# An MLP pair behind top-k attention on one core: second-GEMM products issued by PSUM bank

## The chip, the cores and the metric

The kernel runs on one core of one Trainium2 chip. The metric is the device time of one execution in microseconds. Three runs of the kernel before took 1196.57, 1201.1 and 1203.75 us; the median is 1201.1 us.

## The reference

Attention with a top-32 mask runs over 4 batches, 8 heads, 576 positions and a head size of 64. Its output, 2304 tokens of 512 columns, goes through two MLPs one after the other, each 512 to 2048 to 512: the first with softplus, the second with `h - tanh(h)`.

```python
scores = (q @ k.T) / sqrt(64)
kth = the 32nd largest score of each row
attn = softmax(where(scores >= kth, scores, -1e9)) @ v
x = attn as (2304, 512)
h = x @ moe_w_in;   y = softplus(h) @ moe_w_out
h = y @ moe2_w_in;  out = (h - tanh(h)) @ moe2_w_out
```

All inputs and the output are float32.

## The kernel before

Float32 operands are split into a high and a low float16 part, and each product of the two MLPs becomes three matmuls: high by high, high by low, low by high.

Tokens come in ten chunks: eight of 256 tokens (two per batch, from the plan at line 30) and two of 128, which hold the 64 positions of each batch that are left over. Attention is worked tile by tile, 128 rows of one head at a time: `front` (L1082) makes scores on TensorE and copies them to SBUF on ScalarE, `chain` (L1100) finds the 32 largest on VectorE, `exps`, `mask` and `turn` (L1114 to L1144) make the weights and transpose them by DMA into `pT`, and `back` (L1146) multiplies with the values into the PSUM tile `px`.

Each chunk then has sixteen MLP steps: `m` is 0 or 1 for the first or second MLP, and `g` runs over eight groups of 256 of the 2048 inner columns. `mlp_step` (L1341) calls `gemm1` (L1215, into the PSUM tile `h`), then `act1` (L1232: ScalarE, VectorE for the second MLP, and GpSimd make the two halves of `g`), and puts the step on the list `pend`. `run_gemm2` (L1322) takes it from there three or four steps later and calls `gemm2` (L1254). Gemm2 adds into the accumulators `acc`, PSUM tiles named `y`: two banks for a chunk of 256 tokens, one for 128. In the first MLP a bank holds two blocks of 128 output columns, by 256 tokens; in the second it holds 128 tokens, by all 512 output columns. After `g = 7` the first MLP calls `y_finish` (L1282): ScalarE squares each bank in turn with a running sum, a small matmul adds the sums over partitions, VectorE makes a scale from it, and ScalarE and VectorE write the high and low parts of the next input, bank by bank. The second MLP calls `out_finish` (L1306): a scaled copy of each bank and its DMA out.

The order on each engine is not the order of these calls. A `Recorder` (L149) notes every operation with its cost, its inputs and its outputs, and `order` (L432) lays them out with a model of five engines, in five turns from which the shortest plan is kept; each turn ranks the operations by how late they may start. Everything recorded inside `nc.burst()` (L169) on TensorE is one operation to the planner: it is placed as a whole, starts when all of its inputs are there, and its results count as ready when it ends. TensorE operations that have been ready for 500 ns (`MARG`, L97) come first. On the chip each instruction waits by itself for what it reads. `idle` (L455) adds filler matmuls (L525) in gaps that the plan shows, after 200 us, to hold the clock up. Before about 240 us the kernel also converts the weights, which arrive as float64 words; no gemm2 runs until then.

In gemm2 a burst is one half `fb` (128 inner columns) of a step, over all banks:

```python
for fb in range(2):
    with nc.burst():
        ...
            for d in range(ND):          # m == 0: 4 blocks x 3 matmuls of 256
        ...
            for tt in range(T // P):     # m == 1: 2 banks x 3 matmuls of 512
```

Of the kernel before, what the change touches and what calls it, by code (L numbers as in the profile page):

```python
# [9 lines left out]
F32 = mybir.dt.float32  # L10
F32R = mybir.dt.float32r
BF16 = mybir.dt.bfloat16
F16 = mybir.dt.float16
I32 = mybir.dt.int32
AF = mybir.ActivationFunctionType
ALU = mybir.AluOpType
AX = mybir.AxisListType
# [7 lines left out]
STEP = float(2.0**90)  # L25
# [16 lines left out]
KE = 'P'  # L42
NQH = 1
OWN = 3
MINC = 1
HPW = 100
HPW2 = 0
# [484 lines left out]
def topk_attention_two_mlps(  # L532
# [37 lines left out]
    def al(tag, bufs, shape, dtype, pool=sb, cap=None):  # L570
        s = slots.setdefault(tag, [0, []])
        w = mybir.dt.size(dtype)
        n = math.prod(shape[1:]) * w // 4
        i = s[0] % bufs
        s[0] += 1
        if len(s[1]) <= i:
            s[1].append([pool.tile([P, cap or n], F32, tag=f"{tag}_{i}", name=f"{tag}_{i}"), None])
        s[1][i][1] = Gen(s[1][i][1], s[1][i][0] if pool is pb else None)
        t = View(s[1][i][0][:, 0:n], s[1][i][1])
        t = t if dtype == F32 else t.bitcast(dtype)  # L580
        if len(shape) > 2:
            names = "abcde"[: len(shape) - 1]
            t = t.rearrange(f"p ({' '.join(names)}) -> p {' '.join(names)}", **dict(zip(names, shape[1:])))
        return t
# [21 lines left out]
    def tiny(n=1):  # L606
        o = used_[0]
        used_[0] += n
        return tiles_[:, o : o + n]
# [42 lines left out]
    def xy_take(shape, dtype, name, i=None):  # L652
        if i is None:
            i = xy_free.pop(0)
        return i, al(f"xy{i}", 1, shape, dtype, cap=512)
# [200 lines left out]
    def norm(x, b, s, inv):  # L856
        xf = x[b].rearrange("h s d -> (h s d)").rearrange("(p n) -> p n", p=P)
        n = H * S * D // P
        np_ = -(-n // 512)
        w = n // np_ // 2 * 2  # L860
        ss = al("vss", 2, [P, np_], F32)
        for i in range(np_):
            o, e = i * w, (i + 1) * w if i < np_ - 1 else n
            j, st = xy_take([P, 512], F32, "vst")
            st = st[:, : e - o]
            nc.sync.dma_start(st, xf[:, o:e])
            xy_free.append(j)
            nc.scalar.activation(st, st, AF.Square, accum_out=ss[:, i : i + 1])

        def finish():  # L870
            tot = tiny()
            nc.vector.tensor_reduce(tot, ss, axis=AX.X, op=ALU.add)
            pow2_scale(col_norm(tot, 1), s, inv)
        return finish

    def v_norm(b):

        return norm(v, b, sx[b], ix[b])

    def exp_scale(iq, ik, es, nes, nst):  # L880
        nc.vector.scalar_tensor_tensor(es, iq, QK, ik, op0=ALU.mult, op1=ALU.mult)
        nc.vector.tensor_scalar(nes, es, -1.0, None, op0=ALU.mult)
        nc.vector.tensor_scalar(nst, es, -STEP, None, op0=ALU.mult)
# [10 lines left out]
    def visit_norm(vi):  # L894

        vi.sq, vi.iq, vi.sk, vi.ik, vi.es, vi.nes, vi.nst = (tiny() for _ in range(7))
        ss = al("qss", 1, [P, 2], F32)
        for u, (t, s, inv) in enumerate(((vi.q, vi.sq, vi.iq), (vi.k, vi.sk, vi.ik))):
            j, st = xy_take([P, 2 * D * t.shape[2]], F16, "nst")
            xy_free.append(j)  # L900
            nc.scalar.activation(st, t.rearrange("p j t d -> p (j t d)"), AF.Square, accum_out=ss[:, u : u + 1])
            pow2_scale(col_norm(ss[:, u : u + 1], 1), s, inv)
        exp_scale(vi.iq, vi.ik, vi.es, vi.nes, vi.nst)

    def visit_scales(vi):
# [62 lines left out]
        pass  # L968

    seen = {}  # L970

    def visit_load(b, p, ts, left, twice):
        vi = Visit()
        vi.b, vi.p, vi.ts, vi.left, vi.twice = b, p, ts, left, twice
        nt = len(ts)
        h0 = 2 * p
        vi.kT = []
        vi.again = seen.get((b, p))
        if vi.again is None:
            vi.k = al("kraw", NKR, [P, 2, NB + 1, D], F32)  # L980
            nc.gpsimd.memset(vi.k[SL:P, :, NB, :], 0.0)
            vi.v = al("v", NVR, [P, 2, NB + 1, D], F32)
            for src, dst in ((k, vi.k), (v, vi.v)):
                nc.sync.dma_start(
                    dst[:, :, 0:NB, :],
                    src[b, h0 : h0 + 2, 0 : NB * P, :].rearrange("h (p t) d -> p h t d", t=NB),
                )
                nc.sync.dma_start(dst[0:SL, :, NB, :], src[b, h0 : h0 + 2, NB * P : S, :].rearrange("h s d -> s h d"))

            nc.sync.dma_start(vi.v[SL:P, :, NB, :], v[b, h0 : h0 + 2, NB * P : S, :].rearrange("h s d -> s h d"))  # L990
        if nt:
            vi.q = al("qraw", NQR, [P, 2, nt, D], F32, cap=256)
            for j in range(2):
                nc.sync.dma_start(
                    vi.q[:, j],
                    q[b, h0 + j, 0 : NB * P, :].rearrange("(p t) d -> p t d", t=NB)[:, ts[0] : ts[0] + nt, :],
                )
        if left is not None:
            vi.ql = al("ql", 1, [P, D], F32)
            for j in range(2):  # L1000
                nc.sync.dma_start(vi.ql[j * SL : (j + 1) * SL, :], q[b, h0 + j, NB * P : S, :])
        return vi
# [212 lines left out]
    def gemm1(stp):  # L1215
        m, T, g = stp.m, stp.T, stp.g
        hi, lo = whi[2 * m], wlo[2 * m]
        ps = al("h", NH, [P, 512], F32, pb)
        for fb in range(2):
            with nc.burst():  # L1220
                o = ps[:, fb * T : (fb + 1) * T]
                for d in range(ND):
                    xhi, xlo = stp.x.block(d)[:, 0, :], stp.x.block(d)[:, 1, :]
                    f0 = g * GW + d * 256 + fb * P
                    f = slice(f0, f0 + P)
                    nc.tensor.matmul(o, hi[:, f], xhi, start=(d == 0), stop=False)
                    nc.tensor.matmul(o, hi[:, f], xlo, start=False, stop=False)
                    nc.tensor.matmul(o, lo[:, f], xhi, start=False, stop=(d == ND - 1))
        stp.h = ps[:, 0 : 2 * T]


# [22 lines left out]
    def gemm2(stp):  # L1254
        m, T, g = stp.m, stp.T, stp.g
        hi, lo = whi[2 * m + 1], wlo[2 * m + 1]
        acc = stp.acc
        last = g == NG - 1
        for fb in range(2):
            with nc.burst():  # L1260
                gh, gl = (t[:, fb * T : (fb + 1) * T] for t in (stp.ghi, stp.glo))
                f0 = g * GW + fb * DM
                if m == 0:
                    per = 512 // T
                    for d in range(ND):
                        dd = slice(f0 + d * P, f0 + (d + 1) * P)
                        o = acc[d // per][:, d % per * T : (d % per + 1) * T]
                        first = g == 0 and fb == 0 and d % per == 0
                        fin = last and fb == 1 and d % per == per - 1
                        nc.tensor.matmul(o, hi[:, dd], gh, start=first, stop=False)  # L1270
                        nc.tensor.matmul(o, hi[:, dd], gl, start=False, stop=False)
                        nc.tensor.matmul(o, lo[:, dd], gh, start=False, stop=fin)
                else:
                    f = slice(f0, f0 + DM)
                    for tt in range(T // P):
                        t = slice(tt * P, (tt + 1) * P)
                        first = g == 0 and fb == 0
                        nc.tensor.matmul(acc[tt], gh[:, t], hi[:, f], start=first, stop=False)
                        nc.tensor.matmul(acc[tt], gh[:, t], lo[:, f], start=False, stop=False)
                        nc.tensor.matmul(acc[tt], gl[:, t], hi[:, f], start=False, stop=(last and fb == 1))  # L1280

    def y_finish(ch):  # L1282
        acc = ch.acc1
# [157 lines left out]
    def prep_for(st):  # L1441
        i = st.spec["i"]
        ensure_load(i + 1)
        vi = st.spec["vi"]
        if not vi.kT:
            if i < OWN:
                visit_norm(vi)
            else:
                visit_scales(vi)
            visit_prep_k(vi)  # L1450
            visit_prep_q(vi)
        if st.kind == "l":
            visit_prep_left(vi)
# [66 lines left out]
    NT = len(tiles)  # L1520
    credit = 0.0
    v_norm_at = {12: 1, 40: 2, 56: 3}
    qk_norm_at = {4: 0, 16: 1, 44: 2, 60: 3}

    def emit_steps(n, budget):
        nonlocal_credit[0] += budget
# [39 lines left out]
    for n in range(-1, NT + 2 + BL):  # L1566
# [28 lines left out]
        if 0 <= n + 8 < NT:  # L1595
            ensure_load(tiles[n + 8].spec["i"] + 1)
        if n == VN:
            v_norm(0)()
        if cur is not None and n >= VN and not hasattr(cur.vi, "vdone"):
            with nc.ahead(HP):  # L1600
                visit_prep_v(cur.vi)
# [61 lines left out]
```

## Time and profile before

| what | value |
|---|---|
| median of three runs | 1201.1 us |
| lowest and highest run | 1196.57 and 1203.75 us |
| profiled execution, its own time | 1193.43 us |
| its span | 1191.7 us |
| mean granted clock of TensorE | 0.949 |
| instructions in the profile | 28235 |

The span runs from the first to the last recorded instruction; the time of the same execution has 1.7 us around it. All times in the rows below are microseconds from the start of the span, and a duration is that of one instruction unless a count stands behind it. PE is TensorE's matmuls, PEld its weight loads, DVE is VectorE, ACT is ScalarE, POOL is GpSimd and SP issues DMAs. Neighbouring matmuls overlap in the profile: each row's duration includes the way through the array, so the pace is read from start to start or from the chain. Nearly all instructions carry line 528, the one place from which the recorder emits them, so they are told apart by their tiles.

### The profile page before, as it was taken

To read this page: it belongs to the slowest core of one execution; us is meant where nothing else is said; L and a number is where in the kernel's file an instruction comes from. 1 tells how busy PE (TensorE), PEld (TensorE's weight loads), DVE (VectorE), ACT (ScalarE), POOL (GpSimd) and SP (SyncE) were. 2 spreads that over 40 slices of the span, in tenths; PEclk is the share of its full clock that TensorE was granted. 3 is DMA by queue.
4 is the path that set the end of the run, shared out by engine and by line. 5 is a ranking of instruction groups with operands and counts; after the bars stand their busy time and mean duration, and the time that the engine had idled before them with its cause. 6 is when DMAs were issued, how large, how long until landed. Compare 5 with 4: busy or idle time off the path is not lost.

```text
span 1191.7 us, 28235 instructions
## 1 busy us (share of the span) xinstructions
PE 1050.5 (88%) x10167; PEld 819.7 (69%) x10167; DVE 965.7 (81%) x2116; ACT 912.7 (77%) x1884; POOL 887.2 (74%) x1259
## 2 busy tenths in 40 slices
PE   3477634898998999999999999999998999999998
PEld 2234333787757776787689867986687779977965
DVE  3998999899998999979999989899799898610021
ACT  7999999968998898778887977798568676733332
POOL 3476899899998877857899779787895689643333
PEclk9778865999999999999999999999999999999999
DMA  8977987745589985635775644458555444200000
GB/s 271 283 221 212 263 241 216 176 98 104 110 165 209 186 170 120 138 69 115 145 152 107 139 90 97 88 112 149 107 111 116 78 92 83 52 7 19 1 10 18
DMA packets 322828, 153.18 MB, mean 129 GB/s; under 512 B 270208, under 2 KB 302464, under 8 KB 322688
## 3 DMA queue, kind: packets, MB, share of 16 engines
q1 hardware_dynamic: 322688, 151.39, 55.9%
q8 instruction: 79, 1.29, 0.5%
q14 instruction: 61, 0.50, 0.1%
HBM read 73.04 MB, written 15.37 MB: 74 GB/s over the span
## 4 chain that ended last, share of the span: by engine, by line
PE 37%; DVE 19%; ACT 18%; POOL 9%; DMA 9%; issue 6%; SPq 1%; ACTq 0%; POOLq 0%; DVEq 0%
PE y L528 16%; PE h L528 16%; DVE m L528 8%; DVE x L528 7%; ACT whi L528 3%; DMA pT<-hl 3%; POOL hl L528 3%; ACT ssb L528 2%; ACT x L528 2%; PE px L528 2%; ACT xy L528 2%; ACT wlo L528 2%; PE s L528 2%; ACT hl L528 1%; DMA whi<-in_moe_w_in_dram 1%
## 5 line engine op out<-in xcount | busy, mean ns | idle before, releaser
L528 PEld LDWEIGHTS <-whi 128*128 128x128 f16 x3872 | 360.5, 98 | 69.3 <-issue 13.6
L528 PE MATMUL h<-xy,whi 128*128 128x256 f16 (+1 forms) x2560 | 396.1, 263 | 3.7 <-DMA xy<-xs 2.4
L528 PE MATMUL h<-xy,wlo 128*128 128x256 f16 (+1 forms) x1280 | 325.1, 263 | 0.0
L528 DVE MAX8 m<-x 128x8 f32<-128x576 f32 x432 | 314.6, 745 | 1.6
L528 POOL TENSOR_TENSOR hl<-x,hl 128x512 f16<-128x512 f32 (+1 forms) x288 | 216.1, 769 | 40.1 <-ACT hl L528 26.8
L528 DVE MATCH_REPLACE8 x<-m,x 128x576 f32<-128x576 f32 x288 | 212.6, 739 | 0.0
L528 PEld LDWEIGHTS <-wlo 128*128 128x128 f16 x1920 | 188.2, 98 | 19.8 <-issue 1.9
L528 PE MATMUL y<-g,whi 128*128 128x256 f16 (+1 forms) x1280 | 199.5, 263 | 2.2 <-POOL g L528 1.5
L528 PE MATMUL y<-whi,g 128*128 128x512 f16 x576 | 192.2, 379 | 0.2 <-ACT r L528 0.2
L528 POOL TENSOR_TENSOR g<-r,g 128x512 f16<-128x512 f32 (+1 forms) x160 | 170.5, 1067 | 13.8 <-PE y L528 8.7
L528 PE MATMUL y<-g,wlo 128*128 128x256 f16 (+1 forms) x640 | 162.9, 263 | 0.0
L528 DVE SCALAR_TENSOR_TENSOR r<-h,hinb,r 128x512 f32<-128x512 f32 (+1 forms) x80 | 54.8, 686 | 124.1 <-ACT r L528 124.1
L528 PEld LDWEIGHTS <-g 128*128 128x128 f16 x864 | 83.2, 98 | 75.6 <-issue 0.5
L528 ACT ACTIVATE x<-ssb,nb,tiny 128x576 f32<-128x576 f32 x144 | 124.3, 867 | 14.1 <-DVE m L528 10.9
L528 DVE MAX8 m<-ssb 128x8 f32<-128x576 f32 x144 | 107.5, 747 | 16.6 <-ACT ssb L528 16.3
L528 PEld LDWEIGHTS <-pT 128*128 128x128 f16 (+1 forms) x2240 | 89.0, 102 | 46.2 <-DMA pT<-hl 20.4
L528 PE MATMUL px<-vhl,pT 128*128 128x65 f16 (+1 forms) x2240 | 96.4, 197 | 25.8 <-ACT x L528 12.7
L528 ACT CAST hl<-x 128x576 f16<-128x576 f32 x144 | 96.5, 670 | 22.4 <-POOL x L528 18.6
L528 PE MATMUL s<-kT,qT 128*128 128x288 f16 x512 | 89.3, 300 | 26.0 <-ACT ssb L528 19.5
L528 PE MATMUL y<-wlo,g 128*128 128x512 f16 x288 | 109.2, 379 | 0.0
L528 DVE MATCH_REPLACE8 x<-m,ssb 128x576 f32<-128x576 f32 x144 | 106.4, 739 | 0.0
L528 POOL TENSOR_SCALAR r<-r,gsb 128x512 f32<-128x512 f32 (+1 forms) x80 | 52.4, 655 | 66.5 <-ACT g L528 59.9
(137 smaller groups left out, 1886.8 us busy)
## 6 DMA issues: line engine op xcount, KB each, us to landing
whi<-in_moe_w_in_dram SPq DMA_DIRECT2D x8, 1024.0 KB, 6.5
wlo<-in_moe_w_in_dram SPq DMA_DIRECT2D x6, 1024.0 KB, 6.9
vd<-vhl SPq DMA_DIRECT2D x16, 330.0 KB, 3.7
vhl<-vd SPq DMA_DIRECT2D x16, 330.0 KB, 3.2
kd<-kT SPq DMA_DIRECT2D x32, 160.0 KB, 2.4
whi<-in_moe_w_out_dram SPq DMA_DIRECT2D x5, 1024.0 KB, 5.7
wlo<-in_moe_w_out_dram SPq DMA_DIRECT2D x5, 1024.0 KB, 5.2
kT<-kd SPq DMA_DIRECT2D x32, 160.0 KB, 3.0
```

The source lines that it names most:

```text
L528: fn(*a, **k)
```

## The change

In gemm2 the products are first listed as parts, each with a half `fb`, a bank `i` and the blocks in it. For 256 tokens there are four parts of 6 matmuls (first MLP) or 3 (second); for 128 tokens two of 12 or 3. In the last step of a chunk (`g = 7`) the list is sorted by bank. With `SPB = 2` each part is a burst of its own. The start flag of a bank is still set on its first product and the stop flag on its last.

Other edits of the diff are governed by constants. `OWN0`, `V0`, `EXQ` and `NSL` are 0, which leaves the former path; `G1B = 4` with `ND = 4` leaves gemm1's bursts at four blocks. In `visit_norm` the sum for k goes to column 2 of a buffer of three rather than column 1 of two; the branch for leftover rows is for visits with leftovers, which the first three visits, the only ones that come here, don't have.

```diff
+G1B = 4
+SPB = 2
...
 def gemm1(stp):
...
         for fb in range(2):
-            with nc.burst():
-                o = ps[:, fb * T : (fb + 1) * T]
-                for d in range(ND):
+            o = ps[:, fb * T : (fb + 1) * T]
+            for d0 in range(0, ND, G1B):
+                with nc.burst():
+                    for d in range(d0, min(ND, d0 + G1B)):
...
 def gemm2(stp):
...
-        for fb in range(2):
+        if m == 0:
+            per = 512 // T
+            parts = [(fb, i, range(i * per, (i + 1) * per)) for fb in range(2) for i in range(len(acc))]
+        else:
+            parts = [(fb, i, (i,)) for fb in range(2) for i in range(len(acc))]
+        if SPB and last:
+            parts.sort(key=lambda x: x[1])
+        runs = [[x] for x in parts] if SPB == 1 and (last or g == 0) or SPB == 2 else \
+            [[x for x in parts if x[0] == fb] for fb in range(2)] if not (SPB and last) else [[x for x in parts if x[1] == i] for i in range(len(acc))]
+        for run in runs:
             with nc.burst():
...
+                for fb, i, ds in run:
+                    gh, gl = (t[:, fb * T : (fb + 1) * T] for t in (stp.ghi, stp.glo))
+                    f0 = g * GW + fb * DM
+                    for d in ds:
+                        start, stop = g == 0 and fb == 0 and d == ds[0], last and fb == 1 and d == ds[-1]
+                        if m == 0:
+                            dd = slice(f0 + d * P, f0 + (d + 1) * P)
+                            o = acc[i][:, d % per * T : (d % per + 1) * T]
+                            nc.tensor.matmul(o, hi[:, dd], gh, start=start, stop=False)
+                            nc.tensor.matmul(o, hi[:, dd], gl, start=False, stop=False)
+                            nc.tensor.matmul(o, lo[:, dd], gh, start=False, stop=stop)
+                        else:
+                            f = slice(f0, f0 + DM)
+                            t = slice(i * P, (i + 1) * P)
+                            nc.tensor.matmul(acc[i], gh[:, t], hi[:, f], start=start, stop=False)
+                            nc.tensor.matmul(acc[i], gh[:, t], lo[:, f], start=False, stop=False)
+                            nc.tensor.matmul(acc[i], gl[:, t], hi[:, f], start=False, stop=stop)
```

## Rows read from the trace of the kernel before

**Rows 1.** The page: busy time by engine, and the granted clock in 40 slices.

```profile
...
PE 1050.5 (88%) x10167; PEld 819.7 (69%) x10167; DVE 965.7 (81%) x2116; ACT 912.7 (77%) x1884; POOL 887.2 (74%) x1259
...
PEclk9778865999999999999999999999999999999999
...
```

**Rows 2.** Busy time in stretches: length, PE, PEld, DVE, ACT, POOL, clock, DMA, GB/s.

```profile
...
290.20:300.90 10.70, 9.34 (x95) 7.17 (x93) 10.68 (x27) 10.15 (x25) 10.25 (x17) 0.84 0.79 158
300.90:417.70 116.80, 106.75 (x1039) 83.39 (x1036) 110.85 (x250) 104.76 (x232) 102.86 (x159) 0.99 0.79 168
417.70:426.70 9.00, 7.18 (x79) 5.73 (x77) 8.54 (x25) 9.00 (x21) 6.76 (x18) 0.81 0.85 143
426.70:530.20 103.50, 101.25 (x978) 80.40 (x976) 95.45 (x222) 82.25 (x179) 79.33 (x111) 1.00 0.58 124
530.20:538.10 7.90, 5.79 (x58) 4.43 (x57) 7.56 (x21) 7.17 (x16) 4.30 (x9) 0.78 0.33 70
538.10:909.60 371.50, 362.00 (x3861) 291.20 (x3860) 348.66 (x741) 293.48 (x596) 309.85 (x463) 1.00 0.59 117
909.60:917.90 8.30, 6.56 (x86) 5.38 (x84) 8.30 (x23) 6.82 (x16) 2.90 (x7) 1.00 0.69 121
917.90:1030.00 112.10, 112.10 (x1207) 92.47 (x1205) 97.95 (x205) 77.74 (x155) 86.68 (x118) 1.00 0.40 81
1030.00:1187.60 157.60, 157.13 (x1415) 119.52 (x1412) 23.47 (x47) 58.79 (x101) 63.25 (x85) 1.00 0.06 14
sum 947.60, PE 913.57 PEld 729.37 DVE 759.26 ACT 684.96 POOL 713.71; mean PE 91.36 PEld 72.94 DVE 75.93 ACT 68.50 POOL 71.37
...
```

**Rows 3.** Groups of instructions by form, TensorE, 240 to 1192 us: the fillers.

```profile
...
L525 PE MATMUL h<-tiny 128*128 128x256 bf16 x103 | 15.8, 305 | 0.0
...
L525 PE MATMUL px<-tiny 128*128 128x256 bf16 x39 | 5.5, 274 | 0.0
...
```

**Rows 4.** The chain of work that ended last, 1050 to 1192 us: start, length, what.

```profile
...
1127.90 1.31 PE y L528 x12
...
1177.23 9.73 PE y L528 x45
...
```

**Rows 5.** Timeline, 417.5 to 426.9 us: start, duration, engine, instruction.

```profile
...
417.56 0.27 PE L528 MATMUL y<-g,wlo 128*128 128x256 f16 x1
...
418.31 0.78 ACT L528 ACTIVATE ssb<-ssb,m 128x576 f32<-128x576 f32 x1
...
418.99 0.67 ACT L528 ACTIVATE xy<-y,icab 128x512 f16<-128x512 f32 x1
...
419.65 0.68 ACT L528 ACTIVATE xy<-y,icab 128x512 f16<-128x512 f32 x1
...
420.47 0.38 PE L528 MATMUL px<-yss,tiny 128*128 128x1 f32 x2 [0.29 <-ACT xy L528]
...
423.37 1.27 ACT L528 ACTIVATE xy<-y,sc 128x512 f16<-128x512 f32 x2
...
425.18 1.40 DVE L528 SCALAR_TENSOR_TENSOR xy<-y,sc,xy 128x512 f16<-128x512 f32 x2
...
426.71 0.38 PE L528 MATMUL h<-xy,whi 128*128 128x256 f16 x2
...
```

**Rows 6.** Timeline, 909 to 911 us: another end of a first MLP.

```profile
...
909.48 0.27 PE L528 MATMUL y<-g,wlo 128*128 128x256 f16 x1
909.48 0.67 ACT L528 ACTIVATE xy<-y,icab 128x512 f16<-128x512 f32 x1
...
910.14 0.68 ACT L528 ACTIVATE xy<-y,icab 128x512 f16<-128x512 f32 x1
...
```

**Rows 7.** TensorE's waits, 240 to 1192 us: total, times, longest.

```profile
...
PE px L528 <- DMA pT<-hl: 10.3, 13, 2.6
PE s L528 <- ACT ssb L528: 8.4, 10, 2.2
...
```

**Rows 8.** Timeline, 1186.5 to 1192 us: the output copies.

```profile
...
1187.04 1.33 ACT L528 ACTIVATE r<-y,icb 128x512 f32<-128x512 f32 x2 [6.68 <-PE y L528]
...
```

More of the change, by code (lines that the diff above doesn't have):

```diff
@@ L44 @@
 OWN = 3
+OWN0 = 0
+V0 = 0
+EXQ = 0
+G1B = 4
+NSL = 0
+NSB = 1
+SPB = 2
 MINC = 1
@@ L866, in norm @@
             nc.sync.dma_start(st, xf[:, o:e])
-            xy_free.append(j)
+            xy_free.insert(NSL - 1 if NSL and b >= NSB else len(xy_free), j)
             nc.scalar.activation(st, st, AF.Square, accum_out=ss[:, i : i + 1])
@@ L880, in exp_scale @@
     def exp_scale(iq, ik, es, nes, nst):
+        if EXQ:
+            nc.gpsimd.tensor_scalar(es, iq, ik, QK, op0=ALU.mult, op1=ALU.mult)
+            nc.gpsimd.tensor_scalar(nst, es, -STEP, 1.0, op0=ALU.mult, op1=ALU.mult)
+            nc.gpsimd.tensor_scalar(nes, es, -1.0, 1.0, op0=ALU.mult, op1=ALU.mult)
+            return
         nc.vector.scalar_tensor_tensor(es, iq, QK, ik, op0=ALU.mult, op1=ALU.mult)
@@ L896, in visit_norm @@
         vi.sq, vi.iq, vi.sk, vi.ik, vi.es, vi.nes, vi.nst = (tiny() for _ in range(7))
-        ss = al("qss", 1, [P, 2], F32)
+        ss = al("qss", 1, [P, 3], F32)
+        left = vi.left is not None
+        if vi.again is not None:
+            vi.sk, vi.ik = None, vi.again[2]
+        if left:
+            j, st = xy_take([P, D], F16, "nst")
+            xy_free.append(j)
+            nc.scalar.activation(st, vi.ql, AF.Square, accum_out=ss[:, 1:2])
         for u, (t, s, inv) in enumerate(((vi.q, vi.sq, vi.iq), (vi.k, vi.sk, vi.ik))):
+            if t is None:
+                continue
             j, st = xy_take([P, 2 * D * t.shape[2]], F16, "nst")
             xy_free.append(j)
-            nc.scalar.activation(st, t.rearrange("p j t d -> p (j t d)"), AF.Square, accum_out=ss[:, u : u + 1])
-            pow2_scale(col_norm(ss[:, u : u + 1], 1), s, inv)
+            nc.scalar.activation(st, t.rearrange("p j t d -> p (j t d)"), AF.Square, accum_out=ss[:, 2 * u : 2 * u + 1])
+            n = 2 if u == 0 and left else 1
+            pow2_scale(col_norm(ss[:, 2 * u : 2 * u + n], n), s, inv)
         exp_scale(vi.iq, vi.ik, vi.es, vi.nes, vi.nst)
@@ L970, in topk_attention_two_mlps, with first_v_load @@
     seen = {}
+    first_v = []
+    if V0:
+        for p in range(NP):
+            if p == 0:
+                x = al("v", NVR, [P, 2, NB + 1, D], F32)
+            else:
+                c = NG * GW - 2 * 2 * (NB + 1) * D * p
+                x = wlo[2][:, c : c + 2 * 2 * (NB + 1) * D].bitcast(F32).rearrange("p (h t d) -> p h t d", h=2, t=NB + 1)
+            first_v.append(x)
+    def first_v_load():
+        ss = al("vss", 2, [P, NP], F32, cap=5)
+        for p in range(NP):
+            dst = first_v[p]
+            nc.sync.dma_start(dst[:, :, 0:NB, :],
+                              v[0, 2 * p : 2 * p + 2, 0 : NB * P, :].rearrange("h (p t) d -> p h t d", t=NB))
+            for r in (slice(0, SL), slice(SL, P)):
+                nc.sync.dma_start(dst[r, :, NB, :], v[0, 2 * p : 2 * p + 2, NB * P : S, :].rearrange("h s d -> s h d"))
+            j, st = xy_take([P, 2 * (NB + 1) * D], F16, "vst")
+            xy_free.append(j)
+            nc.scalar.activation(st, dst.rearrange("p h t d -> p (h t d)"), AF.Square, accum_out=ss[:, p : p + 1])
+        tot = tiny()
+        nc.vector.tensor_reduce(tot, ss, axis=AX.X, op=ALU.add)
+        pow2_scale(col_norm(tot, 1), sx[0], ix[0])
     def visit_load(b, p, ts, left, twice):
@@ L978, in visit_load @@
         vi.again = seen.get((b, p))
+        vi.k = None
         if vi.again is None:
@@ L981, in visit_load @@
             nc.gpsimd.memset(vi.k[SL:P, :, NB, :], 0.0)
-            vi.v = al("v", NVR, [P, 2, NB + 1, D], F32)
-            for src, dst in ((k, vi.k), (v, vi.v)):
+            vi.v = first_v[p] if b == 0 and V0 else al("v", NVR, [P, 2, NB + 1, D], F32)
+            for src, dst in ((k, vi.k),) if b == 0 and V0 else ((k, vi.k), (v, vi.v)):
                 nc.sync.dma_start(
@@ L988, in visit_load @@
                 nc.sync.dma_start(dst[0:SL, :, NB, :], src[b, h0 : h0 + 2, NB * P : S, :].rearrange("h s d -> s h d"))
-            nc.sync.dma_start(vi.v[SL:P, :, NB, :], v[b, h0 : h0 + 2, NB * P : S, :].rearrange("h s d -> s h d"))
+            if b or not V0:
+                nc.sync.dma_start(vi.v[SL:P, :, NB, :], v[b, h0 : h0 + 2, NB * P : S, :].rearrange("h s d -> s h d"))
         if nt:
@@ L1219, in gemm1 @@
         for fb in range(2):
-            with nc.burst():
-                o = ps[:, fb * T : (fb + 1) * T]
-                for d in range(ND):
[L1223 to L1228, printed above, removed]
+            o = ps[:, fb * T : (fb + 1) * T]
+            for d0 in range(0, ND, G1B):
+                with nc.burst():
+                    for d in range(d0, min(ND, d0 + G1B)):
+                        xhi, xlo = stp.x.block(d)[:, 0, :], stp.x.block(d)[:, 1, :]
+                        f0 = g * GW + d * 256 + fb * P
+                        f = slice(f0, f0 + P)
+                        nc.tensor.matmul(o, hi[:, f], xhi, start=(d == 0), stop=False)
+                        nc.tensor.matmul(o, hi[:, f], xlo, start=False, stop=False)
+                        nc.tensor.matmul(o, lo[:, f], xhi, start=False, stop=(d == ND - 1))
         stp.h = ps[:, 0 : 2 * T]
@@ L1258, in gemm2 @@
         last = g == NG - 1
-        for fb in range(2):
-            with nc.burst():
[L1261 to L1280, printed above, removed]
@@ new lines, in gemm2 @@
+        for run in runs:
+            with nc.burst():
+                for fb, i, ds in run:
[9 more added lines that the diff above has]
+                            nc.tensor.matmul(o, lo[:, dd], gh, start=False, stop=stop)
+                        else:
+                            f = slice(f0, f0 + DM)
[3 more added lines that the diff above has]
+                            nc.tensor.matmul(acc[i], gl[:, t], hi[:, f], start=False, stop=stop)
@@ L1445, in prep_for @@
         if not vi.kT:
-            if i < OWN:
+            if i < OWN or OWN0 and vi.b == 0:
                 visit_norm(vi)
@@ L1522, in topk_attention_two_mlps @@
     v_norm_at = {12: 1, 40: 2, 56: 3}
-    qk_norm_at = {4: 0, 16: 1, 44: 2, 60: 3}
+    qk_norm_at = {16: 1, 44: 2, 60: 3} if OWN0 else {4: 0, 16: 1, 44: 2, 60: 3}
     def emit_steps(n, budget):
@@ L1597, in topk_attention_two_mlps @@
         if n == VN:
-            v_norm(0)()
+            if V0:
+                first_v_load()
+            else:
+                v_norm(0)()
         if cur is not None and n >= VN and not hasattr(cur.vi, "vdone"):
```

## Prediction

> **What bounds the kernel now.** I read the page first [rows 1]: TensorE is busy 88% of the span and its clock is granted in full nearly everywhere after the first fifth. Then I cut the time after 240 us into stretches [rows 2]. The products that the change touches all run in that time. From 917.9 us on TensorE is busy 112.1 of 112.1 us and 157.13 of 157.6 us, and from 538.1 to 909.6 us it is 362.0 of 371.5 us. VectorE, which finds the top-32 values, is nearly as full up to about 1030 us and then falls to 23.47 of 157.6 us. So the second half is a queue of TensorE work that never empties, and the end moves by what TensorE loses before it. Over 240 to 1187.6 us it idles 947.6 - 913.57 = 34.0 us, and issues 103 + 39 filler matmuls beside it [rows 3].
>
> Is a busy TensorE really full? In the chain of work that ended last, 45 products of 512 columns take 9.73 us (216 ns each) and 12 of 256 columns take 1.31 us (109 ns each) [rows 4]. At 2.4 GHz 512 columns are 213 ns and 256 are 107 ns, so there is no room between them. The work itself does not shrink with the change: as many matmuls and weight loads as before. Only idle time, fillers and clock can be gained.
>
> Where does it go idle? Four stretches in [rows 2] stand out: 290.2 to 300.9, 417.7 to 426.7, 530.2 to 538.1 and 909.6 to 917.9 us, 35.9 us together with 28.87 us of busy time, much of it fillers. Each lies between the last y product of a chunk's first MLP step and the first h product of its second step, when no other chunk has work ready. One of them in detail [rows 5]: the last y product starts at 417.56 us and ends 0.27 us later, at 417.83. ScalarE squares bank 0 at 418.99 and bank 1 at 419.65, the column sum follows at 420.47, the scaled copies at 423.37, VectorE's residues at 425.18, and the first h product at 426.71: 8.9 us after the last y product ended.
>
> **The change, part by part.** It does one thing that acts: the planner's atomic runs of gemm2 for 256-token chunks become half as long, 6 products of 256 columns (0.65 us instead of 1.31) in the first MLP and 3 of 512 columns (0.65 instead of 1.30) in the second [rows 4]. In the last step of a chunk all products of bank 0 come before those of bank 1. The two 128-token chunks have one bank, so their runs stay as they are. Bursts of gemm1 hold four blocks before and after, the new constants at 0 leave their branches unused, the free list is appended to as before, and one column of a small statistics buffer changes its place: nothing for any of these. No DMA is added or moved past another on SP's queue, no wait is added, and POOL's work is the same; POOL's two operations per step still come before the run.
>
> (a) Bank 0 earlier at a chunk's end. Before, bank 0 gets its last product 6 products (0.65 us) ahead of the end; after, 12 products (1.31 us). That the chip lets the square of bank 0 start by itself shows at 909.48 us, where it starts while the last y product is still starting [rows 6]. At 417.7 us it did not: an attention operation that started at 418.31 stood ahead in ScalarE's queue [rows 5]. The planner counts a burst as done when its last product is, so to it bank 0 was ready only with bank 1. With runs by bank it knows better. The least gain is that the first square and its sum (418.99 to 419.65, 0.66 us) leave the chain, if ScalarE finds the place; the most is that plus the wait from 417.83 to 418.99, 1.82 us; below nothing if the square pushes the attention's copy in front. I take 0.9 us, nearer to the 0.66 since that needs no reordering, at three of the four ends; at the fourth the square is early already, and the second can start when that product ends, 909.48 + 0.27 = 909.75, instead of 910.14: 0.4 us. Together 3 x 0.9 + 0.4 = **3.1 us** (0 to 5.9). At the other ends of 256-token chunks h products of another chunk cover it: nothing there, or the same 0.9 if that cover is gone.
>
> (b) The clock. In the first three stretches the granted share is 0.84, 0.81 and 0.78 [rows 2]. With two levels, 1.2 and 2.4 GHz, that is 0.16 x 2 x 10.7 = 3.4 us at the lower one, and as much in the others. Half of each, 1.7 us, is lost where real work runs in it. Before each drop TensorE had too little ready but fillers. A shorter stretch can save one: **1.7 us** (0 to 5.1), an estimate of one in three.
>
> (c) Attention matmuls behind gemm2. A score or output product that becomes ready waits for the run in front, now 0.65 us at most. VectorE gets its scores that much earlier, and the plan has twice the places to put them. The waits of TensorE that this could ease are those for pT and for the score copy, 10.3 + 8.4 = 18.7 us [rows 7]. Most of them are the order's guess being off and stay. I take a tenth, **1.9 us**, between 0 and half (9.4), and as far on the loss side for the reason given under the rivals.
>
> (d) The next chunk's first products can enter bank 0 while bank 1 is still read. While one chunk's bank is evacuated h runs and attention cover it; nothing, or one evacuation (0.67 us) if they are gone. (e) The end: the two output copies take 1.33 us from 1187.04 [rows 8]. Bank 0's copy moves forward, but bank 1's waits for the last product as now: 0.1 us, nothing.
>
> Sum: 3.1 + 1.7 + 1.9 = 6.7 us. The profiled execution took 1193.4 us, 7.7 below the median of the three runs, 1201.1, and below the lowest of them. I apply the sum to the median: 1201.1 - 6.7 = **1194.4 us**; against the profile's own time it would be 1186.7.
>
> **The rivals.** First, the forecast itself, faster by over 0.5%: the chunk ends shorten, and the idle time of 34.0 us falls to under 29. Its own range is 1186 to 1195.
>
> Second, no change that counts. ScalarE is full in the dry stretches: 10.15 of 10.7, 9.0 of 9.0, 7.17 of 7.9 us [rows 2]. A square that moves forward then pushes an attention copy back, and the products that wait for that copy fill the same stretch anyway. Only the fourth end's 0.4 and part of (c) remain, about 2 us: 1199. Against it: the attention operations moved back are not on the way to the first h product. That the change has no effect at all, because the planner puts the halves back to back again, belongs here: 1201.
>
> The Trainium skill (Perfetto Trace Analysis, section Identifying the Most-Contended Engine) holds matmul busy time to be a poor measure of how full TensorE is, and would have headroom judged by weight-load busy time. By that, 119.52 of 157.6 us after 1030 us would leave a quarter free, TensorE would catch up whatever it lost, and the sum would be zero: 1201. The row of 45 products without a gap [rows 4] speaks against it, so it gets 0.03 inside this case.
>
> Third, slower. TensorE takes its instructions in order. Each boundary between runs is a place where the planner may put a score or output product as soon as its model calls the inputs ready (it keeps a margin of 500 ns, the constant MARG). Where the real pT transfer comes later than that, TensorE stands while ready y and h products queue behind it, and ScalarE and VectorE wait for them in turn. The 18.7 us of [rows 7] are such waits. Gemm2 has twice the boundaries now. If the idle time grows by a third, it costs 34.0 / 3 = 11.3 us: 1212. The 13 + 10 waits of those rows are 0.81 us each in the mean, so it takes 14 more of them. Eight chunks of 16 steps get two new boundaries a step, 256 in all: the case decides once one in eighteen of them stalls, that is where pT or the score copy comes later than planned by more than the margin. For it: these waits are already the largest that TensorE has after 240 us. Against it: earlier scores also make VectorE, and so pT, earlier.
>
> **How the numbers follow.** A measurement of this kernel can tell about 0.5%, 6 us, from no change: faster is under 1195.1, slower over 1207.1. The forecast case has 0.45; no change 0.36, of it 0.04 for no effect at all and 0.03 for the busy measure; slower 0.19. The forecast lies close to the bound, so the two first cases are near each other. The range takes the forecast's lower bounds, with all three terms near their better ends (3.1 + 5.1 + 9.4 = 17.6 would be 1183.5), down to 1185, and reaches over no change into a mild loss, 1208. Most of the slower case, and a little below, is left out. Cases of both signs hold 0.64, so the likeliest one's own range stands with it above.
>
> **What would show it.** In the profile after: the square of bank 0 starts before the last y product of the chunk ends, at all four ends; the way from that product to the first h product falls from about 9 to 8 us; fillers under 142; fewer stretches at the lower clock; TensorE idle under 29 us over the same time. In runs of y products 6 or 3 at a time between attention products one sees the halves used. Wrong: TensorE's idle time unchanged with the squares early (the second case), or its waits for pT and score copies above 18.7 us (the third). A change before 240 us, where no product of gemm2 runs, would be the planner's reordering alone and none of these terms.

## The result and the profile after

The changed kernel takes 1189.53 us in the median of twelve runs (1184.65 to 1192.89), the kernel before 1200.18 us in twelve runs (1193.01 to 1203.75). The ratio is 0.9913, with a 95% interval from 0.9891 to 0.9935: 10.7 us, or 0.9%, faster. The forecast was 1194.4 us in a range of 1185 to 1208.

The profiled executions are only 4.4 us apart, 1189.07 against 1193.43 us, since the execution profiled before is nearly the fastest of its kernel. What follows from one pair of traces must be read with that in mind.

The page of the changed kernel: the span, the busy time by engine and the granted clock in 40 slices, as in [rows 1].

```profile
span 1187.0 us, 28134 instructions
...
PE 1044.8 (88%) x10121; PEld 814.4 (69%) x10121; DVE 957.4 (81%) x2116; ACT 911.4 (77%) x1884; POOL 892.7 (75%) x1259
...
PEclk9779855899999999999999999999999999999999
...
```

46 matmuls fewer have been issued, all of them fillers: 193 in the whole kernel instead of 239. The other 9928 products are the same. The same stretches as in [rows 2], cut at the changed kernel's own chunk ends:

```profile
...
288.40:300.20 11.80, 9.06 (x75) 6.85 (x74) 11.80 (x31) 10.42 (x26) 10.04 (x20) 0.71 0.77 162
...
415.20:424.10 8.90, 5.83 (x68) 4.55 (x68) 8.79 (x24) 8.90 (x23) 6.61 (x17) 0.81 0.64 139
...
525.80:533.80 8.00, 4.75 (x67) 3.45 (x66) 7.99 (x24) 7.17 (x17) 3.51 (x8) 1.00 0.74 134
533.80:904.10 370.30, 361.40 (x3869) 290.64 (x3866) 343.39 (x734) 291.50 (x591) 310.85 (x462) 1.00 0.60 115
904.10:912.10 8.00, 6.03 (x57) 4.78 (x56) 8.00 (x20) 7.75 (x19) 4.22 (x10) 0.79 0.54 109
912.10:1025.00 112.90, 112.55 (x1211) 92.31 (x1209) 103.36 (x220) 79.85 (x160) 88.32 (x124) 1.00 0.47 88
1025.00:1182.90 157.90, 157.79 (x1427) 120.47 (x1424) 23.19 (x46) 60.08 (x101) 62.72 (x83) 1.00 0.06 13
sum 946.60, PE 913.70 PEld 730.00 DVE 757.52 ACT 686.27 POOL 716.92; mean PE 91.37 PEld 73.00 DVE 75.75 ACT 68.63 POOL 71.69
...
```

From the first gemm2 product to the last the kernel before took 947.6 us and idled 34.0 [rows 2]; now it is 946.6 us, with 946.6 - 913.7 = 32.9 idle. So in this pair only about 1 us was gained where gemm2 runs. The rest lies ahead of it. The rows that tell when the y products of the first MLP began, before and after (tile `y`, high part: count, shortest, median and longest in ns, first and last start):

```profile
...
L528 PE MATMUL y<-g,whi x1280: 216/273/422, 240.3 to 1128.8; 128*128 128x256 f16 x147, 128*128 128x128 f16 x36
...
```

```profile
...
L535 PE MATMUL y<-g,whi x1280: 216/272/290, 236.3 to 1123.8; 128*128 128x256 f16 x147, 128*128 128x128 f16 x36
...
```

They begin 4.0 us earlier, at 236.3 instead of 240.3, though before that no instruction is new; of the fillers, 42 stand ahead of it instead of 97. The four dry stretches, on the other hand, are 11.8, 8.9, 8.0 and 8.0 us, 36.7 together, against 35.9 before. The square of bank 0 comes early in the first and the third of them and late in the other two. In the second, nearly as before, ScalarE squares bank 0 (416.29) only 1.0 us after the last y product has ended (415.01 + 0.27):

```profile
...
415.01 0.27 PE L535 MATMUL y<-g,wlo 128*128 128x256 f16 x1
...
416.29 0.67 ACT L535 ACTIVATE xy<-y,icab 128x512 f16<-128x512 f32 x1
...
416.95 0.67 ACT L535 ACTIVATE xy<-y,icab 128x512 f16<-128x512 f32 x1
...
421.23 1.26 ACT L535 ACTIVATE xy<-y,sc 128x512 f16<-128x512 f32 x2
...
424.11 0.38 PE L535 MATMUL h<-xy,whi 128*128 128x256 f16 x2
...
```

In the third it starts at 525.57, just after the last product has started, where the square before came 1.0 us after its end. First the rows before, then those after:

```profile
...
530.12 0.27 PE L528 MATMUL y<-g,wlo 128*128 128x256 f16 x1
...
531.42 0.68 ACT L528 ACTIVATE xy<-y,icab 128x512 f16<-128x512 f32 x1
...
536.95 1.41 DVE L528 SCALAR_TENSOR_TENSOR xy<-y,sc,xy 128x512 f16<-128x512 f32 x2 [0.24 <-ACT xy L528]
...
538.13 0.38 PE L528 MATMUL h<-xy,whi 128*128 128x256 f16 x2
...
```

```profile
...
525.53 0.27 PE L535 MATMUL y<-g,wlo 128*128 128x256 f16 x1
...
525.57 0.68 ACT L535 ACTIVATE xy<-y,icab 128x512 f16<-128x512 f32 x1
...
526.24 0.68 ACT L535 ACTIVATE xy<-y,icab 128x512 f16<-128x512 f32 x1
...
531.58 1.41 DVE L535 SCALAR_TENSOR_TENSOR xy<-y,sc,xy 128x512 f16<-128x512 f32 x2
...
533.40 0.60 PE L535 MATMUL px<-vhl,pT 128*128 128x65 f16 x14 [1.30 <-DMA pT<-hl]
...
533.84 0.38 PE L535 MATMUL h<-xy,whi 128*128 128x256 f16 x2
...
```

Counted from the end of the last y product, VectorE's first residue starts 0.8 us sooner than before (5.8 us instead of 6.6), but the first h product comes 0.3 us later (8.0 instead of 7.7): it stands behind an attention product for which TensorE waited 1.30 us, by the trace for pT's DMA. It is much the same at the first dry end:

```profile
...
288.12 0.69 ACT L535 ACTIVATE xy<-y,icab 128x512 f16<-128x512 f32 x1
...
288.21 0.27 PE L535 MATMUL y<-g,wlo 128*128 128x256 f16 x1
...
295.60 4.76 PE L532 MATMUL h<-tiny 128*128 128x256 bf16 x24
...
297.17 1.39 DVE L535 SCALAR_TENSOR_TENSOR xy<-y,sc,xy 128x512 f16<-128x512 f32 x2
...
300.20 0.38 PE L535 MATMUL h<-xy,whi 128*128 128x256 f16 x2
...
```

The residue starts 8.7 us after the last y product instead of 9.8, and the first h product, behind 24 fillers, 11.7 us after it instead of 10.5. At the fourth end the square is late now (905.64, where the last y product has ended at 904.15), and was early before [rows 6].

Fillers and TensorE's two largest waits after the first gemm2 product, to be held against [rows 3] and [rows 7]:

```profile
...
L532 PE MATMUL h<-tiny 128*128 128x256 bf16 x93 | 14.5, 310 | 0.0
L532 PE MATMUL px<-tiny 128*128 128x256 bf16 x58 | 6.8, 274 | 0.0
...
```

```profile
...
PE px L535 <- DMA pT<-hl: 12.0, 13, 2.1
PE s L535 <- ACT ssb L535: 5.5, 8, 1.4
...
```

From there on there are 151 fillers instead of 142, and the two waits come to 17.5 us instead of 18.7.

### The profile page after: what moved, and what is told of

It is laid out like the page before. It is cut to its first block, busy times and chain, and to the rows that moved or that the text cites. A ratio compares the mean times of both kernels' runs of the same rounds, so it can differ in the third digit from the quotient of the medians.

```text
span 1187.0 us, 28134 instructions
## 1 busy us (share of the span) xinstructions
PE 1044.8 (88%) x10121; PEld 814.4 (69%) x10121; DVE 957.4 (81%) x2116; ACT 911.4 (77%) x1884; POOL 892.7 (75%) x1259
## 4 chain that ended last, share of the span: by engine, by line
PE 28%; ACT 17%; POOL 17%; DVE 16%; DMA 11%; issue 9%; SPq 2%; POOLq 0%; ACTq 0%; DVEq 0%
PE h L535 13%; PE y L535 12%; DVE m L535 6%; DVE x L535 6%; POOL hl L535 4%; POOL g L535 4%; DMA pT<-hl 3%; POOL r L535 2%; ACT x L535 2%; ACT xy L535 2%; ACT whi L535 2%; ACT ssb L535 2%; POOL x L535 2%; PE px L535 2%; SPq L535 2%
## 5 line engine op out<-in xcount | busy, mean ns | idle before, releaser
L535 PE MATMUL y<-whi,g 128*128 128x512 f16 x576 | 197.1, 379 | 2.2 <-ACT r L535 1.5
L535 PEld LDWEIGHTS <-pT 128*128 128x128 f16 (+1 forms) x2240 | 91.5, 103 | 60.6 <-DMA pT<-hl 31.6
L535 ACT COPY ssb<-s 128x576 f32<-128x576 f32 x144 | 91.2, 634 | 5.1 <-POOL x L535 3.7
```

What stands on the lines that cost most here:

```text
L535: fn(*a, **k)
```

## The experiments

All ratios are to runs of the kernel before on the same chip as the experiment, where its median was 1196.3 to 1199.6 us; they come with a 95% interval, which holds the spread of executions and not that of plans. Four theories were in play: A, bank 0's square starts early (term a); C, shorter runs let attention products in sooner (term c); B, any new plan is a throw of the dice, and the one before was a bad throw; D, the gain is made in the 240 us ahead of gemm2. After the first eight runs B was set against E: shorter runs make better plans as a rule.

**The product order alone (e_emit).** The plan of the kernel before, with `SPB = 0`; only where the operations are issued is the second bank's part of a last step's first run held back. The tag of a run has its group `g`, its count of banks and its half.

```diff
...
-                for fn, a, k in o.calls:
+                calls = o.calls
+                if o.tag and o.tag[2] == 7 and o.tag[3] == 2:
+                    n = len(calls) // 2
+                    if o.tag[4] == 0:
...
+                        calls, held = calls[:n], calls[n:]
+                    else:
+                        calls, held = calls[:n] + held + calls[n:], []
+                for fn, a, k in calls:
                     fn(*a, **k)
...
```

> The plan of the kernel before, unchanged for every engine; only at the moment of issuing are the products of a 256-token chunk's last step put in bank order (the second bank's part of the first run is held back until the second run). Theory A, the early square (the prediction's term a): the chip lets bank 0's square start up to 0.65 us earlier at each of the eight ends, so 1 to 3 us are gained, 1197 to 1199 against 1200 for the kernel before. Theory B, the planner (the gain comes from the new plan, not from the product order on the chip): nothing, within 1 us, since ScalarE's order is still that of the old plan. Theory C, shorter runs let attention products in sooner: nothing either.

1196.95 us, ratio 1.0006 (0.9984 to 1.0027): nothing. Theory A's 1 to 3 us are not there. The timeline at the second dry end of this kernel shows why; the last y product ends at 422.14, and ScalarE's queue still holds attention operations, the last of them at 422.57, ahead of the square at 423.25:

```profile
...
421.87 0.27 PE L546 MATMUL y<-g,wlo 128*128 128x256 f16 x1
...
422.57 0.78 ACT L546 ACTIVATE ssb<-ssb,m 128x576 f32<-128x576 f32 x1
...
423.25 0.68 ACT L546 ACTIVATE xy<-y,icab 128x512 f16<-128x512 f32 x1
...
```

At all four dry ends the square starts 0.8 to 1.4 us after the last y product has ended. ScalarE keeps the order of the old plan here, so this run tries the chip's part of theory A alone; the planner's part is tried two runs on.

**Shorter runs without the order by bank (e_nosort).**

```diff
-        if SPB and last:
-            parts.sort(key=lambda x: x[1])
```

> Runs of one bank as in the changed kernel, but the last step of a chunk keeps the old order of products (half 0 of both banks, then half 1 of both). Theory A (early square): the gain of the chunk ends goes, so about a third to a half of the 10.7 us is lost, 1193 to 1195. Theory C (shorter runs): the gain stays, 1189 to 1191. Theory B (any new plan is a throw of the dice): anywhere between 1185 and 1200.

1192.07 us, ratio 0.9962 (0.9943 to 0.9981). Less of the gain is left than C expected, and about what A did, but e_emit speaks against A. One plan can't tell.

**The order by bank without shorter runs (e_sortonly).** Only the last step of a chunk is cut otherwise, into one run per bank.

```diff
-SPB = 2
+SPB = 3
```

> Runs as long as before in all steps (both banks of a half in one run) except the last step of a chunk, which is one run per bank, 12 or 6 products. Theory A (early square): a third to a half of the gain stays, 1195 to 1197. Theory C (shorter runs): no gain, 1199 to 1201. Theory B (dice): anywhere between 1185 and 1200.

1198.06 us, ratio 1.0031 (1.0009 to 1.0054): no gain, if anything slightly slower. That is C's expectation and against A. The trace says more, since here term (a) happens in full: at all four dry ends bank 0's square starts before the last y product has ended. This is the second:

```profile
...
426.83 0.69 ACT L535 ACTIVATE xy<-y,icab 128x512 f16<-128x512 f32 x1
...
427.83 0.27 PE L535 MATMUL y<-g,wlo 128*128 128x256 f16 x1
...
432.84 1.38 DVE L535 SCALAR_TENSOR_TENSOR xy<-y,sc,xy 128x512 f16<-128x512 f32 x2
...
433.17 0.27 PE L535 MATMUL h<-xy,whi 128*128 128x256 f16 x1
...
```

From the end of the last y product to the start of the first residue the four ends take 25.2 us together, against 30.8 in the kernel before and 29.7 in the changed one. The 5.6 us saved at these ends didn't reach the end of the kernel. That this one plan lost as much elsewhere for a reason of its own can't be excluded.

**The kernel before, laid out anew (e_jit346).**

```diff
-            return max(31.0, cols / 2.4 + 2.5), 350.0
+            return max(31.0, cols / 2.4 + 2.5), 346.0
```

> The kernel before with one constant of the planner's model changed, the latency from a TensorE result to another engine, 350 to 346 ns. Nothing of the work and no run length changes; only the order on the engines is laid out anew. Theory B (dice): the time moves by several us, to either side, as much as the change did: outside 1198 to 1202. Theories A and C (the gain is from what the change does to runs and ends): it stays near the kernel before, 1198 to 1202.

1193.79 us, ratio 0.9975 (0.9957 to 0.9992). A constant that has nothing to do with gemm2's runs gives a quarter of a per cent, as B expected in kind, though not in size.

**One MLP alone (e_m0only, e_m1only).** The condition `SPB == 2` becomes `m == 0` or `m == 1`, and so does that of the sorting; the other MLP keeps its runs of both banks in the last step too.

```diff
-        if SPB and last:
+        if m == 0 and last:
...
-        runs = [[x] for x in parts] if SPB == 1 and (last or g == 0) or SPB == 2 else \
-            [[x for x in parts if x[0] == fb] for fb in range(2)] if not (SPB and last) else [[x for x in parts if x[1] == i] for i in range(len(acc))]
+        runs = [[x] for x in parts] if SPB == 1 and (last or g == 0) or m == 0 else \
+            [[x for x in parts if x[0] == fb] for fb in range(2)] if True else [[x for x in parts if x[1] == i] for i in range(len(acc))]
...
```

> Runs by bank and the sorted last step in the first MLP alone; the second MLP keeps its runs of both banks. Theory A (early square): the squares belong to the first MLP, so most of the gain stays, 1190 to 1192. Theory C (shorter runs): half of it, about 1195. Theory B (dice): anywhere between 1185 and 1200.

> Runs by bank and the sorted last step in the second MLP alone, the first MLP as before. Theory A (early square): no squares here, so next to nothing is gained, 1198 to 1200. Theory C (shorter runs): half of the gain, about 1195. Theory B (dice): anywhere between 1185 and 1200.

1186.87 us, ratio 0.9895 (0.9868 to 0.9923), and 1189.15 us, ratio 0.9918 (0.9888 to 0.9949). Each half of the change gives as much as the whole. The second MLP has no squares, so A is out as the main cause: the way to the first residue, at the four dry ends, is even longer in e_m1only than before (34.0 us against 30.8). And as the halves don't add up, neither does C hold as a simple sum.

**The order ahead of gemm2 (e_graft_early, e_graft_late).** The planner operations ahead of the first gemm2 product are taken in the order of the other kernel, the rest in its own (`tag` marks the runs of gemm2, `HEAD` is the other kernel's order); the starts by which fillers are set are worked out again for that order.

```diff
...
+        mine = [o for o in self.ops if not o.tag]
+        head = [mine[int(x)] for x in HEAD.split()]
+        own = set(o.i for o in head)
+        done = head + [o for o in done if o.i not in own]
...
```

> Gemm2 runs as in the kernel before, but everything that the changed kernel issues ahead of its first gemm2 product (1303 planner operations: weight conversion and the first attention tiles) is issued in the changed kernel's order; after that the order of the kernel before holds for what is left. Theory D, the stretch before 240 us: the changed profile was 3.0 us ahead there at equal TensorE work done, and that lead is kept to the end, so this kernel gains 3 us or more, 1194 to 1197. Theory A and C: no gain, 1199 to 1202, or a loss where the two orders don't fit together.

> Gemm2 runs as in the changed kernel, but everything that the kernel before issues ahead of its first gemm2 product (1320 planner operations) is issued in that kernel's order, and then the changed kernel's order holds for what is left. Theory D (the lead is made before 240 us): most of the gain goes, 1196 or more. Theories A and C: most of it stays, 1189 to 1193.

1190.83 us, ratio 0.9933 (0.9909 to 0.9956), and 1189.96 us, ratio 0.9926 (0.9899 to 0.9954). The first keeps the old runs, and yet has most of the gain, as D expected; the second keeps the old early order and has most of it too, against D. Their first y products, in the same view as above:

```profile
...
L638 PE MATMUL y<-g,whi x1280: 217/272/421, 235.3 to 1127.2; 128*128 128x256 f16 x147, 128*128 128x128 f16 x36
...
```

```profile
...
L638 PE MATMUL y<-g,whi x1280: 216/272/290, 239.8 to 1124.6; 128*128 128x256 f16 x147, 128*128 128x128 f16 x36
...
```

The early order does make gemm2 begin 5 us sooner (235.3 against 240.3), and the other start stays at 239.8. But the gain does not need it.

**More plans of both kinds (e_b352, e_b354, e_a346, e_a354).** The same constant at other values, in the kernel before (b) and in the changed one (a).

```diff
-            return max(31.0, cols / 2.4 + 2.5), 350.0
+            return max(31.0, cols / 2.4 + 2.5), 352.0
```

> Another re-laid plan of the kernel before: the planner's latency after a TensorE result is 352 instead of 350 ns, nothing else. Theory B (dice: the kernel before has an unlucky plan, any new plan is 0 to 1% faster): 1188 to 1198 against some 1199, in the mean of the plans of this kind about 0.5% faster. Theory E (the shorter runs make better plans as a rule, beside which a plain re-laying moves the time by some tenths of a per cent to either side): ratio 0.997 to 1.003.

> As the run with 352 ns, with 354 ns. Theory B (dice): ratio 0.990 to 1.000. Theory E (shorter runs as a rule): 0.997 to 1.003.

> The changed kernel with the planner's latency after a TensorE result at 346 instead of 350 ns: another plan with the same runs. Theory B (dice): the ratio to the kernel before is thrown anew, 0.990 to 1.000, in the mean no better than the re-laid plans of the kernel before. Theory E (shorter runs as a rule): it stays at 0.988 to 0.994, clear of the re-laid plans of the kernel before.

> The changed kernel with 354 ns. Theory B (dice): ratio 0.990 to 1.000. Theory E (shorter runs as a rule): 0.988 to 0.994.

The kernel before: 1191.82 us, 0.9963 (0.9940 to 0.9986), and 1194.25 us, 0.9985 (0.9963 to 1.0007). The changed kernel: 1182.47 us, 0.9884 (0.9849 to 0.9919), and 1192.30 us, 0.9968 (0.9948 to 0.9988).

E's ranges hold for e_b354 and e_a346 and miss for e_b352 (just) and e_a354; B's mean of 0.5% faster for the kernel before is missed too.

The three re-laid plans of the kernel before have 0.9974 in the mean, the three of the changed kernel (with its own 0.9913) 0.9922. By these means about 0.26%, 3 us, of the gain is that the plan before was a poor throw, and some 0.5%, 6 us, stay for the runs. The best of the one kind and the worst of the other can't be told apart (0.9963 and 0.9968), so both B and E seem true in part; three throws of each kind don't give the shares more closely. All runs together point the same way: the six plans without shorter runs (e_emit has the plan of the kernel before) have 0.9981 in the mean and the seven with them 0.9924, and in 39 of the 42 pairs the plan with shorter runs has the lower ratio. But not all of these plans are independent throws. e_a346 has the lowest ratio of all, but its interval overlaps that of the changed kernel, and it is another throw of the same dice.

**Where the plans with shorter runs win.** In all fourteen traces I added up TensorE's work without fillers (each product at its columns / 2.4 GHz + 2.5 ns, float32 ones at four times that; 975.8 us in all) and took the times at which 110, 330 and 730 us of it had been issued. Ahead of 110 lies the conversion of the weights; behind 730 VectorE's work runs out.

```
                0-110  110-330  330-730  730-end   fillers 500 to 940 us
whole runs
before          244.3   265.2    429.9    252.3     45
e_emit          244.8   270.0    433.1    252.2     45
e_jit346        239.9   266.4    434.3    252.3     43
e_b352          247.9   263.0    427.2    252.7     28
e_b354          240.6   268.6    430.2    252.4     33
e_sortonly      245.7   268.6    429.6    252.5     28
e_graft_early   239.3   266.4    432.0    252.3     45
mean            243.2   266.9    430.9    252.4     38
shorter runs, in one MLP at least
after           241.3   265.1    428.7    251.9     26
e_a346          243.0   266.1    423.1    252.5     16
e_a354          245.4   268.5    429.0    251.7     17
e_nosort        242.1   269.3    427.8    252.5     29
e_m0only        240.9   267.1    424.1    252.5     16
e_m1only        240.9   267.2    427.4    251.8     39
e_graft_late    243.8   266.8    425.5    251.8     26
mean            242.5   267.1    426.5    252.1     24
```

The last column is the same within 1.0 us, and the first two are so in the mean. The difference is in the third column, from some 510 to 940 us, where TensorE and VectorE are both nearly full [rows 2]: 4.4 us in the mean, with one plan of whole runs among the others (e_b352). Before and e_emit, two executions of one plan, are already 3.2 us apart there, so only the seven against seven carry this. No run tried this stretch alone. e_graft_early, with whole runs, has its gain in the first column instead. TensorE also has fewer fillers in that stretch, 24 in the mean against 38: 45 before, 26 after and 16 in e_m0only. (e_b352 and e_sortonly have 28 with whole runs, e_m1only has 39.) These are the rows, 500 to 940 us, of the three kernels in turn:

```profile
...
L525 PE MATMUL h<-tiny 128*128 128x256 bf16 x34 | 4.9, 292 | 0.0
...
L525 PE MATMUL px<-tiny 128*128 128x256 bf16 x11 | 1.5, 274 | 0.0
...
```

```profile
...
L532 PE MATMUL h<-tiny 128*128 128x256 bf16 x26 | 3.5, 274 | 0.0
...
```

```profile
...
L532 PE MATMUL h<-tiny 128*128 128x256 bf16 x16 | 3.3, 343 | 0.0
...
```

Fourteen fewer at 109 ns [rows 4] are 1.5 us by estimate, a part of the 4.4. The last top-k instruction of VectorE shows the same from the other side. Tile `m` in the kernel before, e_emit, the changed kernel and e_a346; the last number before the semicolon is the last start:

```profile
...
L528 DVE MAX8 m<-x x432: 729/744/762, 33.3 to 1033.3; 128x8 f32<-128x576 f32 x144
...
```

```profile
...
L546 DVE MAX8 m<-x x432: 730/746/762, 32.3 to 1041.9; 128x8 f32<-128x576 f32 x144
...
```

```profile
...
L535 DVE MAX8 m<-x x432: 729/747/764, 32.2 to 1028.1; 128x8 f32<-128x576 f32 x144
...
```

```profile
...
L535 DVE MAX8 m<-x x432: 728/747/762, 32.0 to 1025.7; 128x8 f32<-128x576 f32 x144
...
```

The spans are 1191.7, 1200.1, 1187.0 and 1184.7 us: 158.2 to 159.0 us after that start each time (157.9 to 159.8 in all fourteen traces). So nearly the whole difference is made before it. Why the planner with shorter runs finds an order that gets through this stretch sooner was not tried further; that it can serve an attention product between two half runs fits, but is only argued, not shown.

## Why the prediction was right or wrong

The sign is right and the time lies in the range; the gain is 10.7 us where 6.7 were forecast, nearer to it than to no change. The steps stand less well: the largest of the three terms shows no gain, the second can't be shown, and some 3 us come from a source that the sum lacks. That the sum came out near is in good part luck. None of the signs named for the forecast came in full: the squares are early at two of the four ends, TensorE idles 32.9 us and not under 29, there are 151 fillers and not under 142, and three of the four stretches have the lower clock as before. By these signs alone the run would have been put down to the second rival.

- **What bounds the kernel** held. The part after VectorE's work is as full as before (157.79 of 157.9 us) and as long in all fourteen, within 1.9 us. The rival after the Trainium skill (Perfetto Trace Analysis, Identifying the Most-Contended Engine) took weight loads for the measure of room; they are at 120.47 of those 157.9 us now, and there was still no room. The section names, beside the weight loads, the share of the peak rate; the products that start in this stretch need by estimate 153.3 us for their columns at 2.4 GHz, 97% of it, so by that half of the section TensorE is full, as the rows show.
- **(a) Bank 0 earlier**, 3.1 us, failed, in two steps. The first is that an early bank 0 finds ScalarE free: at two of the four ends of the changed kernel it didn't, and with the order alone at none (e_emit). ScalarE is full at these two, as the second rival said: 8.90 of 8.9 and 7.75 of 8.0 us. The second is that what the square gains is passed on. At the two ends with an early square the first residue came 1.1 and 0.8 us sooner, but the first h product later, behind fillers or an attention product that waited for pT. And where the way to the first residue did get shorter at all four, by 5.6 us together in e_sortonly, the kernel wasn't faster. The second rival's conclusion, no change, doesn't follow either, as the gain comes from elsewhere.
- **(b) The clock**, 1.7 us, is not shown. The first three stretches went from 0.84, 0.81 and 0.78 to 0.71, 0.81 and 1.00, and the fourth from 1.00 to 0.79: less time at the lower clock here, more there. Worked as in the prediction, the four have 13.6 us at the lower level instead of 10.3. From the first gemm2 product to 1185 us the records of the granted clock have 13.7 us at it instead of 17.1, but 23.9 in e_emit, whose plan is that of the kernel before; two executions of one plan differ by more than the change.
- **(c) Attention behind gemm2**, 1.9 us, has the right kind of place but, as far as the runs show its size, was too small. The waits fell by 1.2 us in this pair: for the score copy from 8.4 to 5.5, while that for pT rose to 12.0. The mean over seven plans of each kind puts 4.4 us into the stretch where attention and MLP share TensorE. Of the three terms this is the one that the runs speak for, but that the gain there is attention served sooner is argued and not shown.
- **What was missing** is the planner's throw. The prediction said that a change before 240 us would be reordering alone and none of the terms; 3 to 4 us in the profiled pair are that, and re-laying the kernel before gave 1.8 to 4.4 us without any change of the work (0.9985 and 0.9963 of 1200; the interval of the first includes no change). Part of the sum should have been a spread with no place, of some 0.3% to either side, around the effect of the runs.
- **The third rival**, more stalls at new boundaries, didn't come as a whole: the two waits are no larger (17.5 against 18.7 us), though one of them took what the third dry end had gained, and no plan with shorter runs was slower than the kernel before.

## What to carry to other kernels

Where a planner fixes the order on all engines, a small change of its input is two changes: the one meant, and a new throw of the whole order. Lay the old version out anew a few times, with a constant that should not matter, before the gain of one pair is put down to the edit. And a result that comes early helps only if the engine that takes it up stands in the plan with room at that time, and if what it gains isn't lost to the next wait: follow it in the trace to the end of its chain before it is put into a sum.

## What the runs showed that was not expected

Executions of one order differ more than the effects looked for. The trace before and that of e_emit have the same plan for all engines, but for the products that e_emit holds back, and their ratio is 1.0006, yet the two profiled executions took 1193.4 and 1201.8 us; e_emit lost 4.8 us between 110 and 330 us of work and 3.2 in the next part. Such a pair, read as a change, would have shown a slowdown of 0.7%.

VectorE was busy 965.7 us before and 957.4 after with the same 2116 instructions. The top-k instructions keep their lengths, but 18 that pick the bits of the weights went from 24.0 to 20.1 us and the 59 masks from 48.5 to 44.7. So the same instructions take another time in another order; what lengthened them was not looked into. Over all traces this doesn't go with the time: e_graft_late has 964.0 us and a ratio of 0.9926.
